# Attention and an ELU MLP on one core: the low weight bits join in VectorE's shift, and ten softmax tiles keep their exponentials in PSUM

## The chip, the cores and the metric

One core of a Trainium2 chip runs the whole program: TensorE (PE, weight loads PEld), VectorE (DVE), ScalarE (ACT), GpSimd (POOL), and SyncE (SP), which issues all DMAs. The metric is the device time of one execution in microseconds, the median of several runs.

## The reference, cut to what matters

Attention with normalised queries and keys over 8 batches, 12 heads, 448 positions and 64 channels; its output is the input of a two-layer MLP with an ELU between the layers.

```python
q_n, k_n = rmsnorm(q, g_q), rmsnorm(k, g_k)              # (8, 12, 448, 64)
scores = matmul(q_n, k_n.T) / 8
attn = exp(scores - max(scores)); attn /= sum(attn)
x = matmul(attn, v) -> (3584, 768)                       # 8*448 rows, 12*64 channels
h = x @ w_in                                             # (768, 2048)
g = where(h > 0, h, exp(min(h, 0)) - 1)
out = g @ w_out                                          # (2048, 768)
```

The weights arrive as 64-bit floating-point numbers. The kernel makes a 32-bit number of each and splits it into two 16-bit halves (`hi`, `lo`); queries, keys and values are split too, so that a product is three 16-bit matmuls.

## The kernel before, in words

**Attention tiles.** The scores of two heads (896 rows) are cut into 7 tiles of 128 rows by 448 columns; 8 batches times 6 pairs of heads give 336 tiles, numbered T = 0 to 335. For each tile TensorE makes the scores in a PSUM bank (`s`, line 576, from T = 98 on partly in bursts of four, lines 560 and 565), VectorE takes the row maximum (line 583), ScalarE the exponential with its row sum (line 599), GpSimd or VectorE and then VectorE the reciprocal of the sum (lines 603 and 611). The first 42 tiles are transposed by TensorE against a diagonal (GpSimd makes it in line 615, TensorE multiplies in line 623, ScalarE copies out in line 633). All later tiles are split into two 16-bit halves, `s_hi` on ScalarE (line 643) and `s_lo` on VectorE (line 649), and transposed by a DMA (line 659). The product with the values is line 676.

**Where an exponential lies.** For tiles 42 to 83 it is written over the scores in their PSUM bank, for tiles from 84 on into SBUF, into the areas `w32s`, `wts` and `raws` that the weights no longer need. A bank is free for the scores of tile T + 4 when the last reader of its content is done: `s_lo` where the exponential lies in PSUM, the exponential itself where it goes to SBUF.

**Weights.** Sixteen pieces of `w_in` (128 x 768 numbers) and twenty-four of `w_out` (128 x 512) are converted while the first tiles are computed, until about 260 us. `conv` makes the steps for one piece: a DMA brings 64-bit words into `raw`, seen as two 32-bit words (`raw[:, :, 0]` the lower) or four 16-bit ones (`raw16`). `s_act` (ScalarE, line 250) takes the absolute value of the upper word as a float into `t`. `s_bits` (ScalarE, line 253) makes the three bits that come next below, from the upper half of the lower word. `s_shift` (VectorE, line 258) shifts `t` left by three. `s_join` (VectorE, line 282) puts sign and bits to it, into `w`. Column sums on TensorE (line 155) give a power of two for scaling, `s_high` (GpSimd, lines 298 and 320) and `s_low` (VectorE, lines 303 and 325) the two halves.

**The MLP.** Its matmuls are lines 776 (first layer) and 787 (second layer); ELU and scaling are lines 708 to 733.

**Order.** Every engine runs its instructions strictly in the order in which the program gives them. The order is a table, `SCHED`: for each piece or tile a list of half steps, at which its steps are emitted (`put`, `at`). There are two half steps to a tile. SyncE's DMAs are in this order too.

Of the kernel before, what the change touches and what calls it, by code (L numbers as in the profile page):

```python
# [12 lines left out]
U32 = mybir.dt.uint32  # L13
U16 = mybir.dt.uint16
AF = mybir.ActivationFunctionType
ALU = mybir.AluOpType
# [5 lines left out]
NPAIR = H // 2  # L22
DM, DFF = 768, 2048
NC_, NF = DM // 128, DFF // 128
NJ = 2 * S // 128
NCHUNK = B * NPAIR * NJ
PB = NPAIR * NJ
# [6 lines left out]
def tile_attention_then_elu_mlp(ctx: ExitStack, tc: tile.TileContext, qk, v, v_scan, gg, w_in, w_out, out):  # L34
# [13 lines left out]
    nc = tc.nc  # L48
# [19 lines left out]
    def t_mo():  # L68
# [10 lines left out]
        out=ident, in0=ident, scalar1=2.0**UP, scalar2=None, op0=ALU.mult  # L79
# [52 lines left out]
    p_rooms = [t.bitcast(F16) for t in rooms[NE + 2 : NE + 2 + NP16]]  # L132
    BURST = 4

    def in_burst(p):
        return p >= 2 * NPAIR + 2

    def room(all, width, i):
        n = all.shape[1] // width
        return all[:, i % n * width : i % n * width + width]  # L140

    def small(name, w=1, dt=F32, bufs=2):
        return pool.tile([128, w], dt, tag=name, name=name, bufs=bufs)
# [3 lines left out]
    def upper(t):  # L147

        return t.bitcast(BF16).rearrange("p (n w) -> p n w", w=2)[:, :, 1]

    def column_sums(parts, bank):


        for i, a in enumerate(parts + [tiny]):
            nc.tensor.matmul(bank[:, S:], ones, a, start=i == 0, stop=i == len(parts))

    def largest(bank, e):
        nc.vector.tensor_reduce(out=e, in_=bank[:, S:], axis=AX.X, op=ALU.max)
        return e
# [3 lines left out]
    def ibits(dst, src, s1, op0, s2, op1):  # L163
        nc.vector.tensor_scalar(
            out=dst.bitcast(I32), in0=src.bitcast(I32), scalar1=s1, scalar2=s2, op0=op0, op1=op1
        )
# [53 lines left out]
    def on_pe(fn):  # L220

        late.add(fn)
        return fn
# [7 lines left out]
    def conv(src, i, width, acol, bank, parts):  # L231

        raw = raw_in[i % len(raw_in)] if width == WI_W else room(raws, 2 * width, i)
        raw, raw16 = (r.rearrange("p (n w) -> p n w", n=width) for r in (raw, raw.bitcast(U16)))

        t, w = room(wts, width, i), room(w32s, width, i if width == WI_W else i + 2)
        ws = None

        def load():
            nc.sync.dma_start(
                out=raw, in_=src[i].bitcast(U32).rearrange("p (n w) -> p n w", w=2)
            )

        def s_act():

            nc.scalar.activation(t, raw[:, :, 1].bitcast(F32), AF.Abs, scale=2.0**-112)  # L250

        def s_bits():
            nc.scalar.activation(
                raw16[:, :, 2], raw16[:, :, 1], AF.Copy, scale=0.875 * 2.0**-13, bias=0.49
            )

        def s_shift():
            nc.vector.tensor_scalar(
                out=t.bitcast(U32), in0=t.bitcast(U32), scalar1=3, scalar2=None,
                op0=ALU.logical_shift_left,  # L260
            )

        def s_sums():
            column_sums([upper(t[:, a : a + 64]) for a in range(0, width, 64)], bank)

        def s_scale():
            nonlocal ws
            e = largest(bank, acol)
            ws = small("ws", bufs=4)

            ibits(ws, e, POWER, ALU.bitwise_xor, POWER, ALU.bitwise_and)
            if width == WO_W and i % 12 == 11:
                d = i // 4 - 2
                for r in range(4):
                    rows = slice(32 * r, 32 * r + 32)
                    ibits(
                        a_out[rows, d : d + 3], most[rows, 4 * d + r : 4 * d + 12 : 4],
                        POWER, ALU.bitwise_and, 0, ALU.bitwise_or,
                    )

        def s_join():
            nc.vector.scalar_tensor_tensor(
                out=w.bitcast(U32), in0=raw[:, :, 1], scalar=0x80000007, in1=t.bitcast(U32),
                op0=ALU.bitwise_and, op1=ALU.bitwise_or,
            )

        steps = [load, s_act, s_bits, s_shift, s_join, on_pe(s_sums), s_scale]
        for fn in parts:
            step = lambda fn=fn: fn(w, ws)
            steps.append(on_pe(step) if fn in late else step)  # L290
        loads.add(load)
        return steps

    def conv_in(f):
        hi, lo = (t[f].rearrange("p c n -> p (c n)") for t in (whi, wli))

        def s_high(w, ws):
            nc.gpsimd.tensor_scalar(
                out=hi, in0=w, scalar1=ws, scalar2=0.0, op0=ALU.mult, op1=ALU.add
            )  # L300

        def s_low(w, ws):
            nc.vector.scalar_tensor_tensor(
                out=lo, in0=w, scalar=ws, in1=hi, op0=ALU.mult, op1=ALU.subtract
            )

        return conv(
            w_in, f, WI_W, a_in[:, f : f + 1], sb[4 - f] if f < 2 else mb[1], [s_high, s_low],
        )

    def conv_out(i):
        d, r = divmod(i * 32, 128)
        rows = slice(r, r + 32)
        hi = who[d][:, rows]

        def view(w):
            return w.rearrange("p (n f) -> p n f", n=32)

        def s_high(w, ws):
            nc.gpsimd.tensor_scalar(  # L320
                out=hi, in0=view(w), scalar1=ws, scalar2=0.0, op0=ALU.mult, op1=ALU.add
            )

        def s_low(w, ws):
            nc.vector.scalar_tensor_tensor(
                out=wlo[d][:, rows], in0=view(w), scalar=ws, in1=hi, op0=ALU.mult, op1=ALU.subtract
            )

        return conv(
            w_out, i, WO_W, most[:, i : i + 1], mb[1] if i < 9 else av,  # L330
            [s_high, s_low],
        )
# [104 lines left out]
    def q_swap(p):  # L437
        q = qkt[p]
        for a, z in ((64, 0), (0, 64)):
            nc.sync.dma_start(out=q[z : z + 64, 2], in_=q[a : a + 64, 0])  # L440
        if in_burst(p):
            k = q[:, 1].rearrange("p j n -> p (j n)")
            nc.sync.dma_start(out=k_up[p % 2][64:], in_=k[:64, S:])
# [103 lines left out]
    def rows_of(T):  # L547
        p, j = divmod(T, NJ)
        return (ORDER_B if in_burst(p) else ORDER)[j]
# [37 lines left out]
    def by_pe(T):  # L587


        return T < PB  # L590

    def s_exp(T):
        ps, st = pss[T][:, :S], stats[T]
        e = ps
        if T >= 2 * PB:
            e = es[T] = rooms[T % NE]
        elif by_pe(T):
            e = es[T] = pool.tile([128, 2 * S], F16, tag="p16", name="ex", bufs=3).bitcast(F32)
        nc.scalar.activation(e, ps, AF.Exp, bias=st[:, 0:1], accum_out=st[:, 1:2])  # L599
# [198 lines left out]
    def at(h, fn, *args):  # L798
        tasks.setdefault(h, []).append((fn, args))
# [8 lines left out]
    def put(hs, steps):  # L808
        for h, (fn, *args) in zip(hs, steps, strict=True):
            at(h, fn, *args)  # L810

    at(-18, gains)
    for T in reversed(range(NCHUNK)):
        rows = SCHED["tile"]
        hs = rows[T] if T < len(rows) - 1 else [2 * T + h for h in rows[-1]]
        j = T % NJ
        if in_burst(T // NJ) and j < BURST:
            hs = [h + 1 - 0.5 * j for h in hs]
# [7 lines left out]
    for p in range(NP):  # L826
# [6 lines left out]
        hs = [h + HP * (p - k) for h in SCHED["v"][k]]  # L833
# [3 lines left out]
    for b in range(B):  # L837
        k = min(b, 2)
        hs = [h + HB * (b - k) for h in SCHED["scan"][k]]
# [1 line left out]
        put(hs[VSC : 2 * VSC], [(scan_max, b, i) for i in range(VSC)])  # L841
        put(hs[2 * VSC :], [(fn,) for fn in v_steps(b)])
    for f in range(NF):
        put(SCHED["wi"][f], [(fn,) for fn in conv_in(f)])
    for i in range(4 * NC_):
        put(SCHED["wo"][i], [(fn,) for fn in conv_out(i)])
    for b in range(B):
        k = min(b, 1)
        hs = [h + HB * (b - k) for h in SCHED["m"][k]]
# [60 lines left out]
    for h in range(h + 1, h + 9):  # L910
# [4 lines left out]
SCHED = {  # L915
# [274 lines left out]
```

## Time and profile before

| | |
|---|---|
| median of 3 runs | 1230.0 us (1229.31 to 1232.04) |
| the profiled execution's own time | 1233.26 us |
| span of its profile | 1231.5 us |
| busy: PE, DVE, ACT, POOL | 1180.5, 923.7, 810.6, 526.3 us |
| mean granted TensorE clock | 0.996 of 2.4 GHz |

The span runs from the first to the last instruction of the program; the execution's own time lies 1.8 us above it. A busy time is a sum over the span, so 75% for VectorE says nothing yet of the stage with the weights in it.

### The profile page before, as it was taken

Reading aid. Unit: us, or ns where it says so; the run is one execution under the profiler, and the core shown is the slowest. Engines: PE = TensorE matmul, PEld = TensorE weight load, DVE = VectorE, ACT = ScalarE, POOL = GpSimd, SP = SyncE. Lnnn points to the kernel's source line nnn. Section 1 sums busy time; section 2 is a strip of 40 time slices with the busy share of each in tenths; the row PEclk is TensorE's granted clock in tenths of the full one; section 3 lists DMA queues with packets and bytes.
Section 4 is the critical chain, followed back from the end, with each engine's and each line's share of the span. In section 5 each row is a group of like instructions: output and inputs, shape, how many; then the busy total and the mean of one; then the engine's idle time right before and its main releaser. Section 6 shows DMA issues by size and latency. Waiting matters only on the chain.

```text
span 1231.5 us, 21623 instructions
## 1 busy us (share of the span) xinstructions
PE 1180.5 (96%) x7180; PEld 723.1 (59%) x7180; DVE 923.7 (75%) x2042; ACT 810.6 (66%) x1705; POOL 526.3 (43%) x789
## 2 busy tenths in 40 slices
PE   3788899999999999999999999999999999999998
PEld 2555455775456654675556654665557645675576
DVE  7989999888896689767986689767996699642510
ACT  7899999867675477656775487656775487542310
POOL 4776655644444354444444354444444354320000
PEclk9899999999999999999999999999999999999999
DMA  9765888889677977687768867787668866551000
GB/s 304 224 190 164 199 180 177 166 181 188 125 146 159 189 146 131 144 194 154 138 133 162 191 143 135 142 192 156 139 131 170 186 138 137 115 110 28 1 16 30
DMA packets 405744, 183.24 MB, mean 149 GB/s; under 512 B 368896, under 2 KB 388096, under 8 KB 405632
## 3 DMA queue, kind: packets, MB, share of 16 engines
q1 hardware_dynamic: 405632, 181.86, 67.9%
q8 instruction: 57, 0.93, 0.3%
q14 instruction: 55, 0.45, 0.1%
HBM read 68.35 MB, written 11.01 MB: 64 GB/s over the span
## 4 chain that ended last, share of the span: by engine, by line
PE 72%; DVE 1%; DMA 0%; issue 0%; SPq 0%; ACT 0%; ACTq 0%
PE m L787 21%; PE m L776 19%; PE s L787 10%; PE s L776 9%; PE av L676 6%; PE s L576 3%; PE s L560 2%; PE s L565 1%; DVE p L649 0%; DMA ptall<-p 0%; SPq L659 0%; DVE e L714 0%; DVE e L725 0%; DVE gall L733 0%; DVE st L583 0%
## 5 line engine op out<-in xcount | busy, mean ns | idle before, releaser
L787 PE MATMUL m<-gall,whos 128*128 128x448 f16 x1024 | 278.3, 353 | 0.0
L603 POOL TENSOR_SCALAR st<-st 128x1 f32<-128x1 f32 x294 | 78.9, 268 | 456.5 <-ACT w32s L599 402.1
L583 DVE TENSOR_REDUCE st<-s 128x1 f32<-128x448 f32 x336 | 205.7, 616 | 88.4 <-PE s L576 76.9
L787 PEld LDWEIGHTS <-whos 128*128 128x128 f16 x1536 | 221.9, 145 | 69.7 <-issue 0.7
L776 PE MATMUL m<-x,whi 128*128 128x448 f16 x926 | 253.1, 353 | 0.3 <-DVE e L720 0.3
L776 PEld LDWEIGHTS <-whi 128*128 128x128 f16 x1536 | 149.8, 98 | 136.6 <-issue 2.9
L599 ACT ACTIVATE w32s<-s,st 128x448 f32<-128x448 f32 x252 | 158.3, 628 | 76.0 <-DVE st L583 75.4
L649 DVE SCALAR_TENSOR_TENSOR raws<-w32s,st,raws 128x448 f16<-128x448 f32 x199 | 170.8, 859 | 37.3 <-ACT raws L643 36.4
L787 PE MATMUL m<-gall,wlos 128*128 128x448 f16 x512 | 182.0, 355 | 0.0
L776 PE MATMUL m<-x,wli 128*128 128x448 f16 x463 | 163.6, 353 | 0.0
L643 ACT ACTIVATE raws<-w32s,st 128x448 f16<-128x448 f32 x199 | 130.8, 660 | 13.0 <-ACT raws L643 6.9
L787 PE MATMUL s<-gall,whos 128*128 128x448 f16 x512 | 139.1, 353 | 0.0
L787 PEld LDWEIGHTS <-wlos 128*128 128x128 f16 x768 | 110.6, 144 | 47.1 <-issue 13.1
L576 PE MATMUL s<-qkt 128*64 128x448 f16 (+1 forms) x496 | 111.6, 365 | 16.0 <-DMA qkt<-qkt 5.2
L776 PE MATMUL s<-x,whi 128*128 128x448 f16 x450 | 122.4, 352 | 0.6 <-DVE e L725 0.6
L776 PEld LDWEIGHTS <-wli 128*128 128x128 f16 x768 | 75.1, 98 | 79.1 <-issue 13.3
L730 ACT ACTIVATE gall<-e,ui 128x448 f16<-128x448 f32 x128 | 85.1, 665 | 52.6 <-DVE e L725 52.3
L676 PE MATMUL av<-ptall,vt 128*64 128x448 f16 x924 | 95.2, 353 | 1.6 <-DMA ptall<-p 1.0
L733 DVE SCALAR_TENSOR_TENSOR gall<-e,ui,gall 128x448 f16<-128x448 f32 x128 | 88.9, 695 | 9.2 <-ACT gall L730 8.3
L395 POOL TENSOR_TENSOR nat<-nat,r 128x896 f32<-128x896 f32 (+1 forms) x48 | 84.9, 1769 | 21.0 <-DVE r L385 12.8
L787 PE MATMUL s<-gall,wlos 128*128 128x448 f16 x256 | 90.9, 355 | 0.0
L708 ACT ACTIVATE e<-m,sc 128x448 f32<-128x448 f32 x86 | 53.8, 626 | 48.7 <-PE m L776 48.7
(133 smaller groups left out, 1960.1 us busy)
## 6 DMA issues: line engine op xcount, KB each, us to landing
nat<-in_qk SPq DMA_DIRECT2D x48, 448.0 KB, 4.7
raws<-in_w_out SPq DMA_DIRECT2D x24, 512.0 KB, 4.1
qkt<-qkt SPq DMA_DIRECT2D x96, 112.0 KB, 4.3
out<-y SPq DMA_DIRECT2D x48, 224.0 KB, 2.4
vn<-in_v SPq DMA_DIRECT2D x38, 256.0 KB, 2.9
vscan<-in_v_scan SPq DMA_DIRECT2D x36, 224.0 KB, 3.2
whos<-in_w_in SPq DMA_DIRECT2D x10, 768.0 KB, 6.9
raws<-in_w_in SPq DMA_DIRECT2D x6, 768.0 KB, 7.6
```

What stands on the lines that cost most here:

```text
L395: nc.gpsimd.tensor_tensor(out=n[:, a:], in0=n[:, a:], in1=r[:, a:], op=ALU.mult)
L576: nc.tensor.matmul(ps[r0 : r0 + n, :S], lhs, qq[:, 1, h * S : h * S + S], start=(t == 0), stop=(t == 2),)
L583: nc.vector.tensor_reduce(out=st[:, 0:1], in_=pss[T][:, :S], axis=AX.X, op=ALU.max, negate=True)
L599: nc.scalar.activation(e, ps, AF.Exp, bias=st[:, 0:1], accum_out=st[:, 1:2])
L603: (nc.vector if by_pe(T) else nc.gpsimd).tensor_scalar(out=st[:, 1:2], in0=st[:, 1:2], scalar1=1e-9, scalar2=2.0 ** (UP - 7) if by_pe(T) e ...
L643: nc.scalar.activation(p16[:, :S], e, AF.Copy, scale=stats[T][:, 2:3])
L649: nc.vector.scalar_tensor_tensor(out=p16[:, S:], in0=e, scalar=r, in1=p16[:, :S], op0=ALU.mult, op1=ALU.subtract)
L676: nc.tensor.matmul(av[64 * h : 64 * h + 64, :S], vs[:, h], ps[h], start=(k == 0), stop=(k == len(terms) - 1),)
L730: nc.scalar.activation(g[:, 0], e, AF.Copy, scale=ui)
L733: nc.vector.scalar_tensor_tensor(out=g[:, 1], in0=e, scalar=ui, in1=g[:, 0], op0=ALU.mult, op1=ALU.subtract)
L776: nc.tensor.matmul(ph[:, :S], w[:, c, :], x[:, r, :], start=(c == 0 and i == 0), stop=last)
L787: nc.tensor.matmul(py[:, :S], w, g[:, r, :], start=(f == 0 and i == 0), stop=last)
```

## The change

Three edits. (1) `s_bits` writes its three bits as a 32-bit number over the lower word of `raw`, not as a 16-bit number into the lower half of the upper word; `s_shift` becomes an instruction with two tensor inputs that shifts `t` and takes in these bits with an OR; `s_join` takes the sign alone. So the shift now needs the bits, and the join, which comes later, does not. (2) `bits_first` moves `s_bits` in the order to the half step of `s_shift` where it stood behind it (10 of the 40 pieces). (3) `in_sbuf` is 94, not 84: the exponentials of tiles 84 to 93 stay in PSUM.

```diff
+    in_sbuf = (2 * NPAIR + 2) * NJ - BURST
...
         def s_bits():
             nc.scalar.activation(
-                raw16[:, :, 2], raw16[:, :, 1], AF.Copy, scale=0.875 * 2.0**-13, bias=0.49
+                raw[:, :, 0], raw16[:, :, 1], AF.Copy, scale=0.875 * 2.0**-13, bias=0.49
             )
 
         def s_shift():
-            nc.vector.tensor_scalar(
-                out=t.bitcast(U32), in0=t.bitcast(U32), scalar1=3, scalar2=None,
-                op0=ALU.logical_shift_left,
+            nc.vector.scalar_tensor_tensor(
+                out=t.bitcast(U32), in0=t.bitcast(U32), scalar=3, in1=raw[:, :, 0],
+                op0=ALU.logical_shift_left, op1=ALU.bitwise_or,
             )
...
         def s_join():
             nc.vector.scalar_tensor_tensor(
-                out=w.bitcast(U32), in0=raw[:, :, 1], scalar=0x80000007, in1=t.bitcast(U32),
+                out=w.bitcast(U32), in0=raw[:, :, 1], scalar=0x80000000, in1=t.bitcast(U32),
                 op0=ALU.bitwise_and, op1=ALU.bitwise_or,
             )
...
     def s_exp(T):
         ps, st = pss[T][:, :S], stats[T]
         e = ps
-        if T >= 2 * PB:
+        if T >= in_sbuf:
             e = es[T] = rooms[T % NE]
...
+    def bits_first(hs):
+        return hs[:2] + [min(hs[2], hs[3])] + hs[3:]
...
-        put(SCHED["wi"][f], [(fn,) for fn in conv_in(f)])
+        put(bits_first(SCHED["wi"][f]), [(fn,) for fn in conv_in(f)])
...
-        put(SCHED["wo"][i], [(fn,) for fn in conv_out(i)])
+        put(bits_first(SCHED["wo"][i]), [(fn,) for fn in conv_out(i)])
```

What this does to the order of instructions: TensorE, GpSimd and SyncE keep theirs. VectorE keeps its order too, with another instruction in 40 places. On VectorE, at the first piece of `w_in`, this stood before (`wts` holds `t`, `raws` the words of the weights):

```order
L78 TENSOR_SCALAR ident<-ident 128x128
L258 TENSOR_SCALAR wts<-wts 128x768
L409 TENSOR_TENSOR nat<-nat,gst 128x448
L370 TENSOR_REDUCE ss<-ptall 128x14
L425 TENSOR_TENSOR t_194<-nat,t_194 128x7x64
```

and this stands there now (line numbers are 2 higher):

```order
L78 TENSOR_SCALAR ident<-ident 128x128
L260 SCALAR_TENSOR_TENSOR wts<-wts,raws 128x768
L411 TENSOR_TENSOR nat<-nat,gst 128x448
L372 TENSOR_REDUCE ss<-ptall 128x14
L427 TENSOR_TENSOR t_194<-nat,t_194 128x7x64
```

The shift has kept its place and has a second input, `raws`, which ScalarE writes. On ScalarE, `s_bits` moved in ten places. At the first piece of `w_out` it stood so before, five instructions behind `s_act` (line 250):

```order
L250 ACTIVATE wts<-raws 128x512
L599 ACTIVATE ex,st<-s_67,st 128x448
L633 ACTIVATE ptall<-s_70 112x4x128
L683 ACTIVATE x_126<-av,vs 128x448
L414 ACTIVATE t_1202<-nat 128x7x64
L253 ACTIVATE raws<-raws 128x512
```

and now it follows at once (252 is `s_act`, 255 `s_bits`):

```order
L252 ACTIVATE wts<-raws 128x512
L255 ACTIVATE raws<-raws 128x512
L601 ACTIVATE ex,st<-s_67,st 128x448
L635 ACTIVATE ptall<-s_70 112x4x128
L685 ACTIVATE x_126<-av,vs 128x448
L416 ACTIVATE t_1202<-nat 128x7x64
```

The exponential, the copy-out and the two others behind it now come after the bits. Where the exponentials of tiles 84 to 86 are made, ScalarE had:

```order
L599 ACTIVATE w32s,st<-s_67,st 128x448
L374 ACTIVATE ln<-ss,eps 128x14
L375 ACTIVATE r_3437<-ln 128x14
L599 ACTIVATE w32s,st<-s_68,st 128x448
L643 ACTIVATE p_3448<-s_70,st 128x448
L754 ACTIVATE y<-s_71,ua 128x448
L599 ACTIVATE w32s,st<-s_69,st 128x448
L643 ACTIVATE p_3499<-w32s,st 128x448
```

and has now:

```order
L601 ACTIVATE s_67,st<-s_67,st 128x448
L376 ACTIVATE ln<-ss,eps 128x14
L377 ACTIVATE r_3437<-ln 128x14
L601 ACTIVATE s_68,st<-s_68,st 128x448
L645 ACTIVATE p_3448<-s_70,st 128x448
L756 ACTIVATE y<-s_71,ua 128x448
L601 ACTIVATE s_69,st<-s_69,st 128x448
L645 ACTIVATE p_3499<-s_67,st 128x448
```

The order is the same; the exponential goes back into its bank (`s_67` for `w32s`), and the halves are read from there.

## Rows read from the trace of the kernel before

**Rows 1.** Page, its first line: the span.

```profile
span 1231.5 us, 21623 instructions
```

**Rows 2.** Stretches: PE, PEld, DVE, ACT, POOL busy (instructions), clock, DMA share, GB/s.

```profile
12.00:154.00 142.00, 110.94 (x905) 74.39 (x903) 130.83 (x347) 134.75 (x251) 96.02 (x106) 0.96 0.74 210
154.00:215.00 61.00, 58.41 (x398) 31.61 (x397) 59.59 (x140) 59.45 (x117) 31.45 (x45) 1.00 0.88 180
215.00:277.00 62.00, 61.59 (x396) 44.06 (x393) 51.81 (x119) 43.57 (x94) 32.87 (x52) 1.00 0.84 172
```

**Rows 3.** Waits of PE, 12 to 215 us: total us, times, longest.

```profile
PE s L576 <- ACT gall L633: 5.1, 5, 1.5
```

**Rows 4.** Waits of PE, 215 us to the end.

```profile
PE av L676 <- DMA ptall<-p: 1.0, 2, 0.9
PE s L776 <- DVE e L725: 0.6, 1, 0.6
PE s L576 <- DVE p L649: 0.4, 1, 0.4
```

**Rows 5.** Waits of DVE, 12 to 215 us: first and last of ten rows.

```profile
DVE st L583 <- PE s L576: 3.1, 6, 1.2
...
DVE w32s L282 <- ACT raws L253: 0.2, 1, 0.2
```

**Rows 6.** Timeline of PE at 198.58 us.

```profile
198.58 0.54 PE L776 MATMUL m<-x,whi 128*128 128x448 f16 x2 [0.34 <-DVE e L720]
```

**Rows 7.** Groups by line and shape, ScalarE: busy us, mean ns, idle before.

```profile
L253 ACT ACTIVATE raws<-raws 128x512 uint16<-128x512 uint16 x24 | 32.5, 1364 | 0.0
L253 ACT ACTIVATE whos<-whos 128x768 uint16<-128x768 uint16 x10 | 19.1, 1943 | 0.1
L250 ACT ACTIVATE wts<-raws 128x512 f32<-128x512 f32 x24 | 16.4, 685 | 2.1 <-DMA raws<-in_w_out 2.0
L250 ACT ACTIVATE wts<-whos 128x768 f32<-128x768 f32 x10 | 9.1, 907 | 0.0
```

**Rows 8.** The same view, VectorE: the conversion's instructions.

```profile
L258 DVE TENSOR_SCALAR wts<-wts 128x768 uint32<-128x768 uint32 x16 | 12.0, 752 | 0.0
L258 DVE TENSOR_SCALAR wts<-wts 128x512 uint32<-128x512 uint32 x24 | 11.3, 472 | 0.0
L282 DVE SCALAR_TENSOR_TENSOR w32s<-whos,wts 128x768 uint32<-128x768 uint32 x10 | 9.7, 968 | 0.4 <-ACT whos L253 0.4
L282 DVE SCALAR_TENSOR_TENSOR w32s<-raws,wts 128x512 uint32<-128x512 uint32 x24 | 17.8, 745 | 0.2
L303 DVE SCALAR_TENSOR_TENSOR wli<-w32s,ws,whi 128x768 f16<-128x768 f32 x16 | 16.7, 1045 | 0.4 <-POOL whi L298 0.4
L325 DVE SCALAR_TENSOR_TENSOR wlos<-w32s,ws,whos 128x512 f16<-128x512 f32 x24 | 20.6, 863 | 0.1
```

**Rows 9.** Timeline, first piece of `w_in`: `s_bits` on ACT, `s_shift` on DVE.

```profile
10.40 1.93 ACT L253 ACTIVATE raws<-raws 128x768 uint16<-128x768 uint16 x1
11.16 0.55 DVE L258 TENSOR_SCALAR wts<-wts 128x768 uint32<-128x768 uint32 x1
```

**Rows 10.** Timeline, the last piece whose shift began before its bits ended.

```profile
236.71 2.56 ACT L253 ACTIVATE raws<-raws 128x512 uint16<-128x512 uint16 x2
234.70 0.41 DVE L258 TENSOR_SCALAR wts<-wts 128x512 uint32<-128x512 uint32 x1
```

**Rows 11.** Groups by line and shape, `s_lo`: tiles 42 to 83, tiles 84 to 97.

```profile
L649 DVE SCALAR_TENSOR_TENSOR p<-s,st,p 128x448 f16<-128x448 f32 x42 | 28.0, 673 | 5.7 <-ACT p L643 5.5
L649 DVE SCALAR_TENSOR_TENSOR p<-w32s,st,p 128x448 f16<-128x448 f32 x14 | 12.4, 894 | 2.8 <-ACT p L643 2.8
```

**Rows 12.** Timeline: `s_lo` of tile 86, scores of tile 90, `s_lo` of tile 91.

```profile
293.12 0.99 DVE L649 SCALAR_TENSOR_TENSOR p<-w32s,st,p 128x448 f16<-128x448 f32 x1
294.51 0.54 PE L576 MATMUL s<-qkt 128*128 128x448 f16 x2
309.06 1.93 DVE L649 SCALAR_TENSOR_TENSOR p<-w32s,st,p 128x448 f16<-128x448 f32 x1 [1.19 <-ACT p L643]
```

## The prediction

> **What bounds the kernel now.** I read the span first [rows 1], then the busy time by stretches [rows 2]. From 215 us on TensorE is all but full (61.59 of 62 us in the first stretch), and to the end it waits only three more times, 2.0 us in all [rows 4]. So the time is decided earlier: whatever delays TensorE before 215 us stays, because there is no idle time behind it to make up for it. Between 12 and 215 us TensorE is busy for 110.94 + 58.41 = 169.35 of 203 us. In that stage the weights are converted, and two other engines are nearly full: ScalarE with 134.75 + 59.45 = 194.2 us and VectorE with 130.83 + 59.59 = 190.4 us. The change takes work from the one and gives work to the other, so the question is how much VectorE has to spare. Its 12.6 us of idle time there contain 9.1 us of waits that the trace can name, ten kinds of which the first and the last stand in [rows 5]; the rest are short gaps between instructions. From 154 to 215 us it idles 1.4 of 61 us. The last place of this stage where TensorE waits is at 198.58 us, and it waits for VectorE [rows 6]. I therefore measure how much later VectorE comes to that point. This assumes that TensorE follows VectorE there, as the row says it does.
>
> **The sum is made against the profiled execution**, 1233.26 us (its span is 1.8 us shorter). That execution is 3.3 us above the median of the runs, 1230.0; differences carry over to the median.
>
> **The bits on ScalarE (line 253).** They take 1364 ns for 512 numbers and 1943 for 768. The instruction just ahead of them, line 250, reads the same number of words at the same step, writes 32-bit words side by side, and takes 685 and 907 ns [rows 7]. No row shows a 32-bit write at this step. The price of the new form lies between no gain and that of line 250; I take line 250, the same engine, count and step of reading. That relieves ScalarE by 24 x 0.679 + 16 x 1.036 = 32.9 us, none of which is in the sum by itself: it counts only where VectorE or TensorE waited for ScalarE.
>
> The Trainium skill (ScalarE: Activation LUTs, What ACT_TABLE_LOAD costs) gives an activation with immediate scale and bias 186 ns plus 0.833 ns an element, whatever the type; an estimate from it is 612 and 826 ns. Line 250 lies near that, line 253 at 2.2 and 2.4 times as much, so the row decides that the rule leaves something out. Taken at its word, the rule says that the width of the write is not what costs, and then this edit gains nothing on ScalarE; that is the first rival below. With its price for the new form the relief would be 35.3 us, and the sum the same.
>
> **The shift on VectorE (line 258).** With one tensor input it takes 752 and 472 ns; the join, line 282, has exactly the new form (two tensor inputs, one of them every second word, 32-bit numbers) and takes 968 and 745 [rows 8]. That is 0.216 and 0.273 us more. Up to 198.58 us VectorE runs 33 of the 40 shifts, all 16 wide ones and 17 narrow ones: 3.5 + 4.6 = **8.1 us more**. The upper bound comes from lines 303 and 325 of the same widths, 1045 and 863 ns: 16 x 0.293 + 17 x 0.391 = 11.3. A smaller price than the join's has no reason, the form being the same. The last seven shifts add 1.9 us behind this point, four of them where VectorE has 10 us to spare in 62 [rows 2]; without that cover they would cost those 1.9.
>
> **The shift's new wait.** Pairing the 40 bits with the 40 shifts in the order of the code, 22 shifts began before their bits were done: the first by 10.40 + 1.93 - 11.16 = 1.17 us [rows 9], the last 2.0 us before its bits had even begun [rows 10]. Each would now wait, and with it everything behind it on VectorE: row maxima and reciprocals, for which ScalarE's exponentials, GpSimd's diagonals and then TensorE wait. Two things shorten this. Ten of the 22 had the bits moved ahead in ScalarE's order, and the bits end 0.7 to 1.0 us sooner. Of the twelve others only five are then still late, by 3.2 us together if ScalarE begins them when it did; being less loaded it will begin earlier. I take **2 us more**, between 0 and 6.
>
> **What ScalarE gives back.** Of VectorE's 9.1 us of waits the largest is 3.1 us for scores, the others are mostly for ScalarE's results [rows 5]. With ScalarE a sixth less loaded most should shrink, but not those that start in a DMA or in VectorE's own lateness. I take **5.5 us less**, between 0 and 9.1.
>
> **Tiles 84 to 93 in PSUM.** Their `s_lo` took 894 ns on average with both inputs in SBUF, against 673 with one in PSUM [rows 11]; ten of them give back 2.2 us of VectorE, most of it in one that took 1.93 us [rows 12]. What is late behind it are TensorE's two waits of 0.6 and 1.0 us [rows 4]. I take **1.3 us less**. The price is the bank: the scores of tile T + 4 must now wait for `s_lo` of T. For tile 86 that ended at 294.11 us and the scores of tile 90 began at 294.51, so 0.4 us of slack; if VectorE comes later than that, TensorE waits. Bounds: 2.0 less (all waits behind 215 us) and 1.5 more (0.15 us at each of the ten).
>
> That GpSimd is what stretched these instructions is stated by the Trainium skill (SBUF — State Buffer, Who interferes with whom): a VectorE instruction with two SBUF inputs contends with GpSimd's reads. By it the new shift is exposed too, which the join's own rows already contain.
>
> The join's other constant costs nothing, the instruction being the same; moving the bits ahead puts 0.7 to 0.9 us of ScalarE in front of one exponential each time, which is within the bounds of the wait.
>
> **Sum:** 8.1 + 2.0 - 5.5 - 1.3 = +3.3 us: 1236.6 for an execution like the profiled one, **1233.3** for the median.
>
> **Rivals.** *The bits stay slow.* For: nothing in the trace separates the 16-bit write from the 16-bit read that stays. Then ScalarE gives nothing back, and the shifts wait: the twelve pieces not moved by 10.1 us in all and the ten moved ones perhaps 0.5 each; some of that falls into waits that are there anyway, so about 8: 8.1 + 8 - 1.3 = +14.8, 1245.
>
> *ScalarE is what paces the stage.* For: up to 154 us it is fuller than VectorE (134.75 against 130.83 of 142 us), and TensorE waited 5.1 us for one of its copies alone [rows 3]. Then all of VectorE's waits go, none comes new, and TensorE's last 2.0 us go too: 8.1 - 9.1 - 2.0 = -3.0, 1227.0. It decides for a gain that can be measured where more than 10.6 us of waits vanish in all and no new one comes. Against: from 154 us on VectorE has next to none to lose.
>
> *The two cancel.* VectorE gets back 7.5 us and the new wait costs 0.5: 8.1 + 0.5 - 7.5 - 1.3 = -0.2, 1229.8.
>
> **How the numbers follow.** A measurement of this kernel tells 0.2% (2.5 us) from no change. The forecast, VectorE pacing, gets 0.50, with its own range of 1230.5 to 1237.5 (the wait and the giving back each at half their bounds); of it 0.36 is slower and 0.14 within 0.2%. Slow bits get 0.20, all slower. ScalarE pacing gets 0.13: 0.09 faster, 0.04 same. Cancelling gets 0.17: 0.15 same, 0.01 on each side. Together slower 0.57, same 0.33, faster 0.10. The range goes from 1227.5, which leaves out the better part of ScalarE pacing, to 1245, in the middle of the slow bits.
>
> **What the next profile would show.** Line 255 (the bits) near 685 and 907 ns, or else the first rival. Line 260 (the shift) near 745 and 968 ns. ScalarE busy some 33 us less. Waits of VectorE's shift for the bits of 2 us or less. VectorE still at 97% or more between 154 and 215 us, and TensorE's last wait of that stage 4 to 5 us later than 198.58. `s_lo` of tiles 84 to 93 at 673 ns, and no wait of TensorE for them over 0.5 us. The prediction is wrong if VectorE idles in that stage as much as before (more was given back than I think, or it does not pace), or if the shift waits more than 6 us.

## The result and the profile after

| | before | after |
|---|---|---|
| median | 1230.8 us (1229.31 to 1232.04, 4 runs) | 1247.3 us (1246.71 to 1248.17, 4 runs) |
| busy: PE, DVE, ACT, POOL | 1180.5, 923.7, 810.6, 526.3 us | 1183.0, 936.4, 786.7, 529.6 us |

The ratio is 1.0129 (95% interval 1.0113 to 1.0144): 15.9 us slower by the ratio (16.5 by the medians), where 3.3 were forecast and the range ended at 1245.0. VectorE is 12.7 us busier. ScalarE's busy time falls by 23.9 us, not by some 33. The bits' own rows fall by 32, as forecast, but on ScalarE an instruction begins before a long copy ahead of it has ended (in before one begins at 106.70 us under bits that run to 106.96), and busy time counts such an overlap once.

The stretches of after, to set beside [rows 2]:

```profile
12.00:154.00 142.00, 105.49 (x855) 71.31 (x855) 132.55 (x330) 110.83 (x236) 95.45 (x98) 0.94 0.70 199
154.00:215.00 61.00, 54.93 (x372) 29.28 (x371) 58.33 (x131) 52.00 (x109) 33.01 (x43) 1.00 0.87 181
215.00:277.00 62.00, 58.36 (x381) 39.59 (x380) 55.44 (x118) 41.74 (x92) 30.46 (x47) 1.00 0.70 146
```

TensorE, the first number, does less in each: the stage with the weights lasts longer. ScalarE, the fourth, has 31 + 9 = 40 us to spare up to 215 us, where it had 8.8. VectorE, the third, is as full as before. Of TensorE's waits from 12 to 215 us, those for GpSimd's diagonals grow from 8.2 us (nine) to 16.7 (twelve). The last number but two, TensorE's granted clock, is 0.94 of full speed in the first stretch, where before had 0.96. Such differences cost little here: two runs of e1 below had mean clocks of 1.000 and 0.990 and took 1239.6 and 1240.9 us.

TensorE's timeline at the place of [rows 6], and its later waits for VectorE:

```profile
210.01 0.54 PE L778 MATMUL m<-x,whi 128*128 128x448 f16 x2 [0.72 <-DVE e L722]
...
219.04 0.54 PE L778 MATMUL s<-x,whi 128*128 128x448 f16 x2 [1.41 <-DVE e L722]
225.31 0.54 PE L778 MATMUL m<-x,whi 128*128 128x448 f16 x2 [1.42 <-DVE e L722]
232.84 0.54 PE L789 MATMUL m<-gall,whos 128*128 128x448 f16 x2 [0.81 <-DVE e L722]
```

The matmul of 198.58 us begins at 210.01, 11.4 us later, and TensorE still waits for VectorE. Three further waits for line 722 (720 of before) follow, 3.6 us together, where before had the one at 198.58 us alone: the stage in which VectorE holds TensorE now ends near 233 us.

The groups by line and shape (ScalarE's bits against [rows 7], the shift against [rows 8], `s_lo` against [rows 11]):

```profile
L255 ACT ACTIVATE raws<-raws 128x512 uint32<-128x512 uint16 x24 | 16.2, 681 | 0.0
L255 ACT ACTIVATE whos<-whos 128x768 uint32<-128x768 uint16 x10 | 9.1, 907 | 0.0
...
L260 DVE SCALAR_TENSOR_TENSOR wts<-wts,raws 128x512 uint32<-128x512 uint32 x24 | 16.9, 705 | 5.4 <-ACT raws L255 5.3
L260 DVE SCALAR_TENSOR_TENSOR wts<-wts,whos 128x768 uint32<-128x768 uint32 x10 | 10.3, 1032 | 0.9 <-ACT whos L255 0.9
L260 DVE SCALAR_TENSOR_TENSOR wts<-wts,raws 128x768 uint32<-128x768 uint32 x6 | 8.6, 1439 | 1.2 <-ACT raws L255 1.2
...
L651 DVE SCALAR_TENSOR_TENSOR p<-s,st,p 128x448 f16<-128x448 f32 x52 | 34.7, 674 | 7.0 <-ACT p L645 6.8
```

The bits cost half and less, 681 and 907 ns for 1364 and 1943. The idle time ahead of the shift is new: 5.4 + 0.9 + 1.2 us. VectorE's timeline shows it as seven waits:

```profile
11.44 0.96 DVE L260 SCALAR_TENSOR_TENSOR wts<-wts,raws 128x768 uint32<-128x768 uint32 x1 [0.32 <-ACT raws L255]
59.66 0.96 DVE L260 SCALAR_TENSOR_TENSOR wts<-wts,whos 128x768 uint32<-128x768 uint32 x1 [0.93 <-ACT whos L255]
83.13 1.23 DVE L260 SCALAR_TENSOR_TENSOR wts<-wts,raws 128x768 uint32<-128x768 uint32 x1 [0.88 <-ACT raws L255]
109.81 0.69 DVE L260 SCALAR_TENSOR_TENSOR wts<-wts,raws 128x512 uint32<-128x512 uint32 x1 [1.39 <-ACT raws L255]
196.51 0.69 DVE L260 SCALAR_TENSOR_TENSOR wts<-wts,raws 128x512 uint32<-128x512 uint32 x1 [0.89 <-ACT raws L255]
204.39 0.69 DVE L260 SCALAR_TENSOR_TENSOR wts<-wts,raws 128x512 uint32<-128x512 uint32 x1 [0.63 <-ACT raws L255]
217.70 0.69 DVE L260 SCALAR_TENSOR_TENSOR wts<-wts,raws 128x512 uint32<-128x512 uint32 x1 [2.42 <-ACT raws L255]
```

They sum to 7.5 us. What ScalarE did before the last of them, from its timeline:

```profile
207.72 0.68 ACT L252 ACTIVATE wts<-raws 128x512 f32<-128x512 f32 x1
208.29 0.53 ACT L685 ACTIVATE x<-av 128x448 f16<-128x448 f32 x1
208.72 0.67 ACT L714 ACTIVATE e<-e,one 128x448 f32<-128x448 f32 x1
210.72 0.63 ACT L645 ACTIVATE p<-s,st 128x448 f16<-128x448 f32 x1 [1.33 <-DVE st L613]
...
214.29 0.60 ACT L601 ACTIVATE s<-s,st 128x448 f32<-128x448 f32 x1
...
215.98 0.57 ACT L406 ACTIVATE t<-nat 128x448 f16<-128x448 f32 x1
216.44 1.22 ACT L255 ACTIVATE raws<-raws 128x512 uint32<-128x512 uint16 x2
```

This is the nineteenth piece of `w_out`. Its absolute value was there at 208.4 us, its bits came as the second of the two at the end of the list, at 217.7. `bits_first` had moved them ahead of eight instructions, but only to the half step of the shift; on ScalarE an exponential, halves, copies and ELU steps still stood ahead of them, one of which (210.72) had itself waited 1.33 us for VectorE.

### The profile page after: what moved, and what is told of

It reads as the page before. It is cut to its first block, busy times and chain, and to the rows that moved or that the text cites. A ratio compares the mean times of both kernels' runs of the same rounds, so it can differ in the third digit from the quotient of the medians.

```text
span 1245.8 us, 21638 instructions
## 1 busy us (share of the span) xinstructions
PE 1183.0 (95%) x7180; PEld 723.6 (58%) x7180; DVE 936.4 (75%) x2042; ACT 786.7 (63%) x1705; POOL 529.6 (43%) x789
## 4 chain that ended last, share of the span: by engine, by line
PE 78%; DVE 4%; ACT 1%; issue 1%; DMA 0%; POOL 0%; SPq 0%; ACTq 0%; POOLq 0%
PE m L789 22%; PE m L778 21%; PE s L789 11%; PE s L778 10%; PE av L678 6%; PE s L578 4%; PE s L562 2%; PE s L567 1%; DVE wlos L327 1%; DVE p L651 1%; ACT p L645 0%; DVE st L585 0%; DVE w32s L284 0%; DVE wts L260 0%; DVE e L722 0%
## 5 line engine op out<-in xcount | busy, mean ns | idle before, releaser
L601 ACT ACTIVATE w32s<-s,st 128x448 f32<-128x448 f32 x242 | 152.2, 629 | 72.8 <-DVE st L585 71.8
L397 POOL TENSOR_TENSOR nat<-nat,r 128x896 f32<-128x896 f32 (+1 forms) x48 | 85.0, 1771 | 25.6 <-DVE r L387 16.5
```

The lines of the kernel that those rows point to most:

```text
L397: nc.gpsimd.tensor_tensor(out=n[:, a:], in0=n[:, a:], in1=r[:, a:], op=ALU.mult)
```

## The experiments

Each kernel was timed in five rounds beside the kernel before, whose medians were 1231.5 us for e1 to e4, 1231.5 for e5 to e8 and 1232.0 for e9 to e12. The microseconds in the last column are ratio minus 1, times 1231.5.

| run | median us | ratio (95%) | against before |
|---|---|---|---|
| e1 shift alone | 1240.8 | 1.0070 (1.0057 to 1.0082) | +8.6 |
| e2 relief of ScalarE alone | 1231.9 | 1.0000 (0.9988 to 1.0012) | 0.0 |
| e3 after, shift not waiting | 1239.6 | 1.0060 (1.0048 to 1.0073) | +7.4 |
| e4 tiles alone | 1229.2 | 0.9982 (0.9973 to 0.9990) | -2.2 |
| e5 after again | 1247.5 | 1.0132 (1.0118 to 1.0146) | +16.3 |
| e6 after, all bits early | 1243.3 | 1.0092 (1.0079 to 1.0106) | +11.3 |
| e7 before without shift | 1228.8 | 0.9981 (0.9972 to 0.9990) | -2.3 |
| e8 the same, with the relief | 1227.5 | 0.9968 (0.9956 to 0.9979) | -3.9 |
| e9 before, ScalarE +14.5 us | 1243.4 | 1.0095 (1.0081 to 1.0109) | +11.7 |
| e10 wide pieces alone | 1237.1 | 1.0043 (1.0031 to 1.0056) | +5.3 |
| e11 narrow pieces alone | 1244.1 | 1.0103 (1.0088 to 1.0118) | +12.7 |
| e12 all bits early, no wait | 1243.0 | 1.0094 (1.0080 to 1.0107) | +11.6 |

My theory ahead of them (A) was that VectorE paces the stage, so that its longer shifts and its waits show in full; the rivals stand with the runs. e1, e2, e3, e7, e8 and e12 leave out or change bits of the weights and only measure.

### The parts one by one

**e1, the shift's second input alone**, in the kernel before:

```diff
-            nc.vector.tensor_scalar(
-                out=t.bitcast(U32), in0=t.bitcast(U32), scalar1=3, scalar2=None,
-                op0=ALU.logical_shift_left,
+            nc.vector.scalar_tensor_tensor(
+                out=t.bitcast(U32), in0=t.bitcast(U32), scalar=3, in1=raw[:, :, 0],
+                op0=ALU.logical_shift_left, op1=ALU.bitwise_and,
             )
```

> The kernel before with the two-input shift alone: its second input is the untouched lower word, taken in with an AND instead of the OR (so the weights are not the reference's); the bits, the join, the order and the tiles stay as before, and the shift waits for no bits. Theory A (VectorE paces the stage, and the shift next to GpSimd costs more than I took from the join): the whole of its longer time shows, 11 to 13 us, 1242 to 1244. Rival B (the shift costs what the join's rows say, 8.1 us): 1238 to 1239.5. Rival C (VectorE has cover for most of it, and it was the wait for the bits that cost): under 1235.

1240.8, +8.6: between A (11 to 13) and B (8.1), nearer to B. C falls.

**e2, ScalarE's relief alone**, in the kernel before:

```diff
-                raw16[:, :, 2], raw16[:, :, 1], AF.Copy, scale=0.875 * 2.0**-13, bias=0.49
+                raw[:, :, 0], raw16[:, :, 1], AF.Copy, scale=0.875 * 2.0**-13, bias=0.49
...
-                out=w.bitcast(U32), in0=raw[:, :, 1], scalar=0x80000007, in1=t.bitcast(U32),
+                out=w.bitcast(U32), in0=raw[:, :, 1], scalar=0x80000000, in1=t.bitcast(U32),
```

> The kernel before with the bits written as 32-bit numbers over the lower word and the sign alone in the join; the shift is the old one with one input, so the three bits are left out of the weights. ScalarE has 24 to 33 us less work in the stage and VectorE nothing more. Theory A (VectorE paces): it gets back only its own waits for ScalarE, 3 to 7 us, 1224 to 1228. Rival D (ScalarE paces as much): 10 us or more, 1221 or less. Rival E (what VectorE no longer waits for, it waits for something else): 1229 to 1232.

0.0 us, with an interval of 1.5 to either side: E. The stretch of 12 to 154 us in its trace:

```profile
12.00:154.00 142.00, 112.69 (x917) 74.65 (x914) 134.96 (x355) 120.82 (x258) 100.12 (x111) 0.98 0.78 216
```

ScalarE has 21 us to spare there, VectorE 7. Nothing of ScalarE's relief comes back as time.

**e3, no wait for the bits**, in the kernel after:

```diff
-                out=t.bitcast(U32), in0=t.bitcast(U32), scalar=3, in1=raw[:, :, 0],
+                out=t.bitcast(U32), in0=t.bitcast(U32), scalar=3, in1=raw[:, :, 1],
```

> The kernel after with the shift's second input the upper word, which lies at the same step and is there before the absolute value is taken (the weights are not the reference's): every instruction, its shape and its place are as after, but the shift does not wait for the bits. Theory A (waits of VectorE for the bits are paid in full, 7.4 us of them in the trace of after up to 218 us): 5 to 7.4 us below after, 1240 to 1242. Rival F (the waits only take the place of others, because after and before have the same sum of gaps up to 198 us): within 2 us of after, 1245 to 1247.5.

1239.6. By the ratios, 1.0129 and 1.0132 against 1.0060, the wait costs 0.69 to 0.72%, 8.5 to 8.9 us, give or take 2.4 (the two intervals' halves, in quadrature): A, the seven waits cost what they last. F falls.

**e4, the tiles alone**, in the kernel before:

```diff
-        if T >= 2 * PB:
+        if T >= (2 * NPAIR + 2) * NJ - 4:
```

> The kernel before with only the limit at 94 instead of 84: the exponentials of ten tiles stay in PSUM. As forecast: 1.3 us less, 1229 to 1230 where before has 1230.8, and not below 1228.8. Rival G (the bank comes free too late, and TensorE waits for it): 1231 to 1232.5.

2.2 us faster, the interval 1.2 to 3.3: as forecast and a little more. It is the version to keep: faster than both kernels, with nothing left out. TensorE's waits from 215 us to the end, against [rows 4]:

```profile
PE av L676 <- issue: 0.8, 1, 0.8
PE av L676 <- DMA ptall<-p: 0.3, 1, 0.3
PE s L576 <- DVE p L649: 0.2, 1, 0.2
```

No wait for a bank that came free late has appeared; G falls.

### Is the wait the order's doing?

**e5** is the kernel after once more.

> The kernel after once more, so that the next one is compared with it on one chip: 1246 to 1249.

It came out as expected, at 1247.5. **e6** is after, with the bits right behind the absolute value everywhere:

```diff
-        return hs[:2] + [min(hs[2], hs[3])] + hs[3:]
+        return hs[:2] + [hs[1]] + hs[3:]
```

> The kernel after with the bits right behind the absolute value in ScalarE's order for all 40 pieces; computes what the reference does. Theory A (VectorE paces, and the waits for the bits cost what they last, because bits are queued behind exponentials that wait for VectorE): nearly all waits of the shift for bits go, and the time is that of the kernel without this wait, 6 to 8 us below after, 1239.5 to 1242. Rival F (an exponential moved behind the bits costs as much as the wait): within 2 us of after, 1245 to 1249.

1243.3, between both theories: about half of the wait's price comes back. The longest waits of VectorE from 12 to 230 us in its trace:

```profile
DVE st L585 <- PE s L578: 1.5, 3, 1.0
DVE e L722 <- ACT e L714: 0.9, 1, 0.9
DVE st L605 <- ACT ex L601: 0.8, 2, 0.4
```

No wait for bits is left. So something else costs, and **e12** (e6's order with e3's second input) says what.

> The kernel after with the bits right behind the absolute value in all pieces and the upper word as the shift's second input (the weights are not the reference's): the order of the early bits without any wait for them. If what the early bits leave is the price of the order (exponentials behind the bits), it is the time of the early bits, 1242 to 1244.5. If it is what is left of the waits, it is the time of the kernel without the wait, 1238.5 to 1241.

1243.0, the time of e6: what is left over e3, 3.4 us (4.2 by the ratios, give or take 2.3), is the price of the order. That it is the exponentials behind the bits that cost this is argued, not shown. Moving the bits further ahead removes the waits, but not for nothing.

### What paces the kernel before?

That ScalarE's relief is worth nothing did not fit what I had taken for a close second. **e7** takes the shift out of the kernel before, **e8** also gives ScalarE e2's relief:

```diff
-        steps = [load, s_act, s_bits, s_shift, s_join, on_pe(s_sums), s_scale]
+        steps = [load, s_act, s_bits, lambda: None, s_join, on_pe(s_sums), s_scale]
```

> The kernel before without the shift (the weights are not the reference's): VectorE has 20 us less work up to 198 us and 23.5 us in all, nothing else changes. Theory A (VectorE paces, ScalarE, all but as full, comes next): the time falls by 5 to 12 us, 1219 to 1226, and then TensorE's waits of the stage are for ScalarE. Rival H (each waits for the other, none paces): 1227 or more.

> The kernel before without the shift, and with the bits as 32-bit numbers over the lower word and the sign alone in the join (three bits and the shift left out of the weights). Theory A: where VectorE no longer paces, the relief of ScalarE is worth something: 4 us or more below the kernel without the shift alone. Rival E (what ScalarE gives back is worth nothing anywhere, because it waits for VectorE and TensorE rather than they for it): within 2 us of it.

Without 23 us of VectorE's work [rows 8] the time falls by only 2.3 us, where A expected 5 to 12: rival H. With ScalarE's relief on top it falls by 3.9; that is 1.6 more than in e7, so rival E. Stretches of e7:

```profile
12.00:154.00 142.00, 109.86 (x908) 72.22 (x908) 123.27 (x330) 137.39 (x258) 94.57 (x109) 0.99 0.77 215
154.00:215.00 61.00, 60.07 (x425) 33.19 (x425) 56.49 (x131) 60.27 (x120) 29.56 (x44) 1.00 0.85 176
```

and of e8:

```profile
12.00:154.00 142.00, 115.37 (x926) 76.05 (x926) 126.39 (x336) 122.81 (x266) 96.91 (x111) 0.99 0.77 220
154.00:215.00 61.00, 59.53 (x421) 32.89 (x420) 58.26 (x132) 55.25 (x117) 31.81 (x44) 1.00 0.85 179
```

In e7 ScalarE is full in VectorE's place (137.39 of 142 and 60.27 of 61 us), and TensorE idles as long as before. In e8 neither is full up to 154 us, TensorE still idles 26.6 us there, and then it is nearly full itself.

So a theory J took A's place: the kernel before stands at a corner, where more work on either engine shows and less on one alone does not. (J does not say why e8, with both relieved, gains no more than 3.9 us.) **e9** tests it from the other side, with the absolute value taken twice in the wide pieces:

```diff
-            nc.scalar.activation(t, raw[:, :, 1].bitcast(F32), AF.Abs, scale=2.0**-112)
+            for _ in range(2 if width == WI_W else 1):
+                nc.scalar.activation(t, raw[:, :, 1].bitcast(F32), AF.Abs, scale=2.0**-112)
```

> The kernel before with the absolute value taken twice in each of the 16 wide pieces: ScalarE has 16 x 0.907 = 14.5 us more work up to 105 us, VectorE none. Theory J (before stands where VectorE and ScalarE are both full, so that more work on either shows and less on one alone does not): 6 to 14 us, 1237 to 1245. Theory A (VectorE alone paces): ScalarE has some 8 us of idle time in the stage and follows, under 3 us, 1231 to 1234.5.

+11.7 of 14.5 us: J. TensorE's waits for ScalarE's copies from 12 to 215 us, the first of them to set beside [rows 3]:

```profile
PE s L577 <- ACT gall L634: 8.1, 8, 2.3
PE s L577 <- ACT ptall L634: 6.4, 9, 2.2
```

It waits 8.1 and 6.4 us for the two kinds of copies, where it waited 5.1 and 2.6 in before.

### Wide and narrow pieces

**e10** has the new form in the 16 pieces of `w_in` alone, **e11** in the 24 of `w_out`, with the join's constant and the place of the bits to match and the tiles as before (e10, in part; e11 has `WO_W`):

```diff
+            dst = raw[:, :, 0] if width == WI_W else raw16[:, :, 2]
...
+            if width == WI_W:
+                nc.vector.scalar_tensor_tensor(
+                    out=t.bitcast(U32), in0=t.bitcast(U32), scalar=3, in1=raw[:, :, 0],
+                    op0=ALU.logical_shift_left, op1=ALU.bitwise_or,
+                )
+            else:
```

> The kernel before with the new bits, shift, join and place of the bits in the 16 wide pieces alone; tiles as before. The shift without a wait took 1.03 us (ten) and 1.39 us (six) against 0.752: 6.6 us. Waits for bits at wide pieces were 2.1 us in the trace of after. Theory J (added work and waits of VectorE are paid in full, relief of ScalarE is worth nothing): 7 to 9 us more, 1238 to 1240.5. Rival K (half of the load falls into the slack that the relief of ScalarE opens): under 1236.

> The same for the 24 narrow pieces alone. The shift without a wait took 0.693 us against 0.472: 5.3 us, 1.5 of them at the last seven; waits for bits at narrow pieces were 5.3 us. Theory J: 7 to 10.5 us more, 1238 to 1242, and with the wide pieces together 16 to 18.5 us. Rival K: under 1236.

+5.3 and +12.7, less and more than expected. Together with the tiles (-2.2) that makes 15.8 us: the parts add up. K falls, though for the wide pieces it is near: 1237.1, with K under 1236 and J from 1238. The narrow ones have the longer waits, as the trace of e11 says of its shift:

```profile
L260 DVE SCALAR_TENSOR_TENSOR wts<-wts,raws x24: 666/691/989, 103.2 to 257.9; 128x512 uint32<-128x512 uint32 x24
...
  ACT raws L254: 5.9, 4
```

Four waits hold 5.9 us of it. The shifts add 24 x (0.69 - 0.47) = 5.3, by the median here and the mean in [rows 8].

## Why the prediction was wrong

**What paces (half right).** The argument was that TensorE follows VectorE at 198.58 us, so VectorE's lateness there is the result. In after it does follow, 11.4 us later, and three waits beyond that place add to it. But the argument was used in both directions. Upwards it holds (e1); downwards it does not (e7): 23 us less are worth 2.3.

**"What ScalarE gives back: 5.5 us less" (failed).** e2 measures 0.0, between 1.5 less and 1.5 more. VectorE's waits did shrink: those that the trace names from 12 to 215 us are 9.1 us in before and 4.6 in e2. But the step took the waits of [rows 5] for time that a faster ScalarE would return, and they returned none. Nor did they beside the longer shift: e3, which has the relief, is at 7.4 us, and e1 and e4 without it make 8.6 - 2.2 = 6.4. e8 shows that even with both engines relieved only 3.9 us come back. Part of those waits belonged to that one execution: e4, which changes nothing ahead of tile 84, has 7.0 us of them, and the same matmul as in [rows 6] stands here in its timeline:

```profile
195.89 0.54 PE L776 MATMUL m<-x,whi 128*128 128x448 f16 x2 [0.33 <-DVE e L720]
```

2.7 us earlier, without a cause in the code. (The granted clock from 78 to 84 us was 0.72 in before and 1.00 in e4; no run shows that this is the cause.) The execution of e4 is at its median; that of before was 3.3 us above its first median, and 1.3 to 2.5 above the later ones.

**"The shift's new wait: 2 us more" (failed).** e3 prices it at 8.5 us, beyond the upper bound of 6. The step let only five pieces that were not moved be late, and counted the moved ones as in time. Of the seven waits above, those at 59.66, 109.81, 196.51 and 217.70 us are of pieces whose half step `bits_first` had lowered: 0.93 + 1.39 + 0.89 + 2.42 = 5.6 us. The three others make 1.8, where I had 3.2.

Three of those four were not moved on ScalarE at all. This is ScalarE's timeline at the piece that waits at 109.81 us, the first of `w_out`, in before and then in after, from its absolute value to its bits:

```profile
103.33 0.70 ACT L250 ACTIVATE wts<-raws 128x512 f32<-128x512 f32 x1
103.94 0.57 ACT L633 ACTIVATE ptall<-s 112x512 f32<-112x512 f32 x1
104.52 0.58 ACT L404 ACTIVATE t<-nat 128x448 f16<-128x448 f32 x1
105.00 0.62 ACT L599 ACTIVATE ex<-s,st 128x448 f32<-128x448 f32 x1
...
105.61 1.35 ACT L253 ACTIVATE raws<-raws 128x512 uint16<-128x512 uint16 x1
...
106.49 0.67 ACT L252 ACTIVATE wts<-raws 128x512 f32<-128x512 f32 x1
107.06 0.59 ACT L635 ACTIVATE ptall<-s 112x512 f32<-112x512 f32 x1
108.03 0.58 ACT L406 ACTIVATE t<-nat 128x448 f16<-128x448 f32 x1 [0.38 <-DMA qkt<-t]
108.51 0.62 ACT L601 ACTIVATE ex<-s,st 128x448 f32<-128x448 f32 x1
...
109.12 0.66 ACT L255 ACTIVATE raws<-raws 128x512 uint32<-128x512 uint16 x1
```

The same instructions stand ahead of the bits. `bits_first` lowers the half step of eleven pieces, not ten, and in only seven of them do the bits pass another instruction of ScalarE; the order that the section on the change shows for the first piece of `w_out` is that of the fourth, which is one of the seven and has no wait. In the trace of before the shifts of the four other pieces began 2.11, 2.77, 1.14 and 1.80 us ahead of the end of their bits. With bits that end 0.7 or 1.0 us sooner this leaves 4.7 us (an estimate from these rows) that the step should have counted. And the nineteenth piece, which did move, had the longest wait: a half step puts the bits behind everything that ScalarE has not yet done. The second support, that a less loaded ScalarE begins earlier, fails where what is ahead of the bits waits for VectorE, as at 210.72 us.

**The shift: 8.1 us (right in time, in part by luck).** e1 gives 8.6. The shifts themselves grew more: in after by 16 x 0.43 + 24 x 0.23 = 12.5 us in all (16 at a mean of 1.185, 24 at 0.705, against [rows 8]), where the same step had 8.1 + 1.9 = 10.0. The 33 shifts up to 198.58 us grew by 11.2, where the step had 8.1. It set the join's mean against the shift's mean at 768 numbers, 0.968 against 0.752; but the mean of before held shifts that ran beside GpSimd and took longer:

```profile
L258 DVE TENSOR_SCALAR wts<-wts x40: 406/494/1749, 11.2 to 248.7; 128x512 uint32<-128x512 uint32 x24, 128x768 uint32<-128x768 uint32 x16
```

One took 1.75 us, where [rows 9] has 0.55 for the same size. Such neighbours stay. Not all of the growth reached the end of the stage, so a price that was too low met an overlap that the step did not have.

**Tiles 84 to 93: 1.3 us less.** e4 gives 2.2, with 1.3 in its interval; `s_lo` is at 674 ns as forecast.

**The sum by the runs:** 8.6 (e1) + 8.5 (e3) - 0 (e2) - 2.2 (e4) = 14.9, against 15.9 measured. The forecast of 3.3 misses by 12.6, of which the wait makes 6.5 and the giving back 5.5.

**The rivals.** Slow bits: refuted by line 255, although 1245 lay nearest; this rival had a wait of 8 us and nothing given back, for another reason. ScalarE pacing: refuted by e2. The two cancelling: refuted by both failed steps. With fast bits none of the cases held a long wait together with nothing given back, though the bounds of both terms allowed it: 8.1 + 6 - 0 - 1.3 = 12.8. In the working on the bits, 24 x 0.752 + 16 x 1.117 is 35.9 us, not 35.3; nothing in the sum hangs on it.

**The signs.** Both signs of being wrong came: the shift waits 7.5 us, more than 6, and VectorE idles from 12 to 215 us as long as before (12.1 and 12.6 us). The second was to mean that more was given back or that VectorE does not pace; here the new waits for the bits, 5.0 us up to 215, stand where old ones have gone.

What holds e8 at 1227.5 has not been tried: TensorE idles 26.6 us up to 154 us while neither VectorE nor ScalarE is full. The waits that its trace names for TensorE there are above all for GpSimd's diagonals (10.2 us, eleven waits) and for DMAs of queries and keys (7.9 us, six waits).

## What to carry to other kernels

A wait in a balanced stage is a price when it is added and often none when it is removed: before crediting relief, ask what the waiting engine would do next, and test the direction that you credit. When an instruction gains an input from another engine, pair each with its producer in that engine's own order, moved ones too, and count what stands ahead: an earlier place in the program may pass nothing on that engine, and it does not say when the engine gets there. Compare two forms of an instruction by rows without a disturbing neighbour, and a profile's waits with those of a second execution.

## What the hardware showed unexpectedly

**The width of ScalarE's write.** With the same 16-bit reads at the same step, the copy takes 681 ns instead of 1364 for 512 numbers and 907 instead of 1943 for 768 when it writes 32-bit words. The place changed with the width (the lower word instead of the upper); no run separates the two. The Trainium skill (ScalarE: Activation LUTs, What ACT_TABLE_LOAD costs) gives 186 ns plus 0.833 ns an element with immediate scale and bias; 612 and 826 ns, an estimate from it, lie near the new form and far off the old, and the measurement decides.

**VectorE beside GpSimd.** VectorE's and GpSimd's timelines of after, at the shift of the seventh wide piece and at a tiny instruction:

```profile
47.63 2.15 DVE L260 SCALAR_TENSOR_TENSOR wts<-wts,raws 128x768 uint32<-128x768 uint32 x1
47.27 1.69 POOL L397 TENSOR_TENSOR nat<-nat,r 128x896 f32<-128x896 f32 x1 [0.78 <-DVE r L387]
228.18 1.04 DVE L387 TENSOR_SCALAR r<-r,kap 128x7 f32<-128x7 f32 x1
228.16 1.04 POOL L420 TENSOR_TENSOR t<-nat,t 128x448 f16<-128x448 f32 x1
```

The shift takes 2.15 us and ends 0.82 us after GpSimd's instruction, about as long as it needs alone (0.96 at 11.44 us); the instruction on 7 columns (0.23 us at 46.95 us, and at most 0.23 in before) ends with GpSimd's, within 0.02 us. In both pairs VectorE looks held until GpSimd was through, rather than slowed. The Trainium skill (SBUF — State Buffer, Who interferes with whom) calls the contention between the two engines an exclusive lock; both pairs of rows agree. So a delay on VectorE changes which of its instructions meet GpSimd's, and the lengthening near 228 us is one that no count of instructions shows; what it costs in time has not been measured.
